# Hash and row sums in four column groups, eight hash transfers, and a second queue for one output piece

## The chip, the cores and the metric

The kernel runs on one core of one Trainium2 chip. The metric is the device time of one execution in microseconds (us). TensorE (PE in the profile) multiplies matrices, VectorE (DVE), ScalarE (ACT) and GpSimd (POOL) work on elements, and SyncE (SP), ScalarE and GpSimd start DMA transfers. Matrix results stand in PSUM, everything else in SBUF, both with 128 partitions.

## The reference

Attention in which a query sees only the keys of its own hash bucket, and then a two-layer network. Cut to what matters:

```
B, H, S, D = 4, 8, 768, 64;  proj: [64, 6]
q_bits = (q @ proj > 0);  k_bits = (k @ proj > 0)          # 6 bits for each row
mask   = bucket(q_bits)[..., :, None] == bucket(k_bits)[..., None, :]
scores = where(mask, (q @ k.T) / 8, -1e9)
attn   = softmax(scores);   x = (attn @ v)  ->  [3072, 512]
h = x @ w_in                                                # [3072, 2048]
out = (max(h, 0) + alpha * min(h, 0)) @ w_out               # [3072, 512]
```

All of it is float32 in the reference.

## The kernel before

The work has two blocks. The first is attention and lasts until about 318 us of the profile. It handles 16 pairs of heads (`pairs`, index `pi`), two heads at once: head s = 0 in partitions 0 to 63, s = 1 in partitions 64 to 127. The second is the network, a sequence of products in which seven products stand for eight (`Product`, L882).

The order is written out by hand: `do` keeps every instruction of an engine in the order of the program, so the order of calls in the loop at L1165 is the order on each engine. DMA starts stand on the queue of the engine that starts them: most loads and stores on SyncE, the weight loads `load_weight` (L578) and the hash transfers on GpSimd.

For a pair the loop does, on TensorE:

- `scores` (L760): 12 cells (six blocks of 128 keys times two halves of 384 queries). A cell has two bf16 matmuls of the hash rows (`bits`) and two f32 matmuls of q and k (`tr`), one of each for each head, into a PSUM tile `sc` of two banks. The hash part is 0 where all six bits agree and negative otherwise; ScalarE's Exp (L771) turns the cell into `pts`.
- `hash_bits` for the next pair (L713).
- `attend` (L793): the product with v, in tiles of 128 rows and 32 columns, four side by side, into `av`.
- `totals` (L807): the ones product. Row sums of `pts`, first added up by VectorE (`accp`, `accd`, L779 to L790), are multiplied with a matrix of ones into `sm`.

`two_banks` (L683) gives tiles of two PSUM banks from a ring of three. Scores, hash and totals all take from this ring, so the third cell of a pair gets the buffer of the `sm` tile before it.

On VectorE `divide` (L820) follows in the next pair's time: two transposes of `sm` into `st` (L831), the reciprocals (L834), the copies on GpSimd that exchange the halves (L840, L841), a transpose into `dn` and the product `x` (L849), which goes to DRAM. VectorE also turns q and k of later pairs (`turn_blocks`, L704) and prepares the network's weights (`weight_*`).

The hash in more detail. `wh` holds proj in columns 0 to 5 of a 32-column matrix, for each head in its 64 partitions. For pair `pi + 1`, eight matmuls of 64 rows by 32 columns (two heads, q and k, two halves of 384) fill both banks of one tile; a Sign on ScalarE with bias `hb` writes `kb` (L736), with 6 rows of signs and 6 rows of constants for each head and name. Rows then have to move to the partitions of their head: four transfers of 32 rows for q (L741) and two of 64 rows for k (L743), all started by GpSimd; one half of k is already in place. The first pair is done in another way, by halves, with its own tiles (`engine=DVE`), since its bits are needed at once.

At the end of the network `turn_out` (L1061) transposes a finished piece of the output on VectorE and starts twelve transfers of it on SyncE; `turn_last` (L1077) does the last two pieces with TensorE. A piece is put on the list `to_turn` in a product's last step (step 4). In the last block of the loop `turn_last(0)` is called where the other blocks call `turn_out`, and `turn_last(1)` after the loop.

Of the kernel before, what the change touches and what calls it, by code (L numbers as in the profile page):

```python
# [407 lines left out]
def fast_path(  # L408
# [12 lines left out]
    nc = tc.nc  # L421
# [39 lines left out]
    wh = const.tile([P, 32], F32, name="wh")  # L461
    hb = const.tile([P, 1], F32, name="hb")
    hb_k = const.tile([P, 2], F32, name="hb_k")
    alpha16 = const.tile([NF, P], F32, name="alpha16")
    alpha = const.tile([P, NF], F32, name="alpha")
    mags = const.tile([P, 2, NPAIR], F32, name="mags")

    qbs = [pool.tile([P, S], BF16, name=f"qb{i}", bufs=1) for i in range(2)]
    NI = NF // 2
    NM = 7  # L470
    w_in_s = dram.tile([NI, P, NM, 2, P], F32, name="w_in_s")
# [238 lines left out]
        n = "qk".index(name)  # L710
        do(ACT.activation(t, t, AF.Square, accum_out=mags[:, n, pi : pi + 1]))

    def hash_bits(pi, halves=BOTH, engine=None):  # L713

        if halves.start == 0:
            bits["q", pi] = qbs[pi % 2]
            kb = pool.tile([P, 3 * CW], BF16, name=f"kb{pi}", tag="kb", bufs=1)
            bits["k", pi] = kb[:, :S]  # L720
            bits["raw", pi] = kb.rearrange("p (a w) -> p a w", w=CW)
        ps = {"k": two_banks(f"hs{pi}")}
        ps["q"] = psum_av.tile([P, 2, 512], F32, name=f"hsq{pi}", tag="av") if engine is DVE else ps["k"]
        for half in range(halves.start, halves.stop):
            for name in "qk" if engine is DVE else "kq":
                for s in range(2):
                    r, c = D * s, D * (s ^ half) + 32 * "kq".index(name)

                    for t, c in [("k", c)] + ([("q", c ^ D)] if engine is DVE and name == "q" else []):
                        do(PE.matmul(  # L730
                            ps[t][c : c + 32, half if t == "k" or engine is not DVE else 0, :CW], wh[r : r + D],
                            tr[name, pi][r : r + D, half * CW : (half + 1) * CW], start=True, stop=True,
                        ))
        if engine is None:
            raw = bits["raw", pi]
# [8 lines left out]
            return  # L744
        for half in range(halves.start, halves.stop):
            cols = slice(half * CW, (half + 1) * CW)
            for s in range(2):
                c = D * (s ^ half ^ (engine is DVE)) + 32
                do(ACT.activation(
                    bits["q", pi][D * s : D * s + 32, cols], ps["q"][c : c + 32, 0 if engine is DVE else half, :CW], AF.Sign, bias=hb[c : c + 32],  # L750
                ))

            for to, c, n in [(0, 0, P)] if half == 0 else [(0, D, D), (D, 0, D)]:
                dst, src = bits["k", pi][to : to + n, cols], ps["k"][c : c + n, half, :CW]
                do(DVE.tensor_scalar(
                    dst, src, hb_k[c : c + n, 0:1], hb_k[c : c + n, 1:2], op0=ALU.is_gt, op1=ALU.subtract,
                ))


    def scores(pi, cells):  # L760
# [46 lines left out]
    def totals(pi):  # L807


        sums[pi] = two_banks(f"sm{pi}")  # L810
        for g in range(NCH):
            for s in range(2):
                for h in range(2):
                    r = D * s + 32 * h
                    do(PE.matmul(
                        sums[pi][r : r + 32, g, :HW2], ones, accd[pi][:, NCH * g + s, h * HW2 : (h + 1) * HW2],
                        start=True, stop=True,
                    ))

    def divide(pi, between=lambda: None):  # L820

        b, hp = pairs[pi]
        n = HW2 // 32
        a = pool.tile([P, NCH, HW2], F32, name=f"st{pi}", tag="st", bufs=1)
        r = pool.tile([P, NCH, n], F32, name=f"rc{pi}", tag="rc")
        rr = pool.tile([P, NCH, 2, n], F32, name=f"rr{pi}", tag="rr")
        d = pool.tile([P, NCH, CW], F32, name=f"dn{pi}", tag="dn", bufs=1)
        for g in range(NCH):  # L830
            do(DVE.transpose(a[:, g], sums[pi][:, g, :HW2]))  # L831
        do(DVE.tensor_scalar(r, a.rearrange("p g (n w) -> p g n w", w=32)[:, :, :, 0], S * EPS, None, op0=ALU.add))
        for h in range(2):
            do(DVE.reciprocal(rr[:, :, h], r))  # L834
        vsum[pi] = pool.tile([P, 1], F32, name=f"vs{pi}", tag="vs")
        do(DVE.tensor_scalar(vsum[pi], av[pi][:, 0, CW : CW + 1], EPS, None, op0=ALU.mult))
        weight_sums(1, vsum[pi])
        for q0 in (0, D):
            q1 = q0 + 32
            do(POOL.tensor_copy(rr[q0 : q0 + 32, :, 1], rr[q1 : q1 + 32, :, 1]))  # L840
            do(POOL.tensor_copy(rr[q1 : q1 + 32, :, 0], rr[q0 : q0 + 32, :, 0]))  # L841
        between()
        do(DVE.transpose(
            d.rearrange("p g w -> p (g w)"),
            rr.rearrange("p g h n -> p (g h n)").unsqueeze(2).to_broadcast([P, 2 * NCH * n, 32]),
        ))
# [295 lines left out]
    for half in (first, second):  # L1142
        turn(0, "q", half)
        turn(0, "k", half, DVE)
        if half is first:
            nil[0]()
            hash_bits(0, first, DVE)
    load(1, "q")
    load(1, "k")
    load_weight(0, nc.sync)  # L1150
# [178 lines left out]
```

## Time and profile before

| what | value |
| --- | --- |
| median of 3 runs | 875.19 us (874.47 to 875.37) |
| profiled execution, own time | 874.04 us |
| its span | 872.3 us |
| granted TensorE clock | 0.998 of full speed |
| TensorE busy | 861.0 us, 99% of the span |
| VectorE busy | 748.5 us, 86% |
| ScalarE busy | 366.8 us, 42% |
| GpSimd busy | 116.2 us, 13% |
| matmul records of the hash (L730) | 256, 29.2 us counted by record |
| matmul records of the ones product (L815) | 256, 13.5 us |
| Sign of the hash (L736) | 15, 901 ns each |
| transposes of the sums (L831) | 32, 343 ns each |
| issues of hash transfers (L741, L743) | 60 at 504 ns and 30 at 520 ns |

A line of the timeline gives the start and the length in us, engine, source line, operation, output<-input, and a count. A matmul of f32 leaves two records. "64*128" before a shape is the tile of TensorE (rows by columns); matmuls in different tiles may run side by side, and a length of 0.81 for four records is the time from the first start to the last end. "Idle before" is the time an engine stood still before an instruction, with what ended it. A wait in the list of waits has the total, the count and the longest.

### The profile page before, as it was taken

What the parts mean: (1) busy time and instruction counts of PE and PEld (TensorE: products, weight loads), DVE (VectorE), ACT (ScalarE), POOL (GpSimd) and SP (SyncE); (2) the same over time, 40 slices, a digit from 0 to 9 for tenths busy, and PEclk for the clock granted to TensorE, in tenths of its full rate; (3) what the DMA queues carried; (4) which work ended last, traced back from release to release, by engine and by line L of the source; (5) the groups of instructions that cost most, each with busy time, mean ns of one, the idle gap of its engine ahead of it and who ended that gap; (6) DMA issues with size and microseconds to landing.
All of it is one profiled execution on the core that took longest, in us unless ns stands there. A gap on an engine that the chain in (4) does not pass through costs nothing.

```text
span 872.3 us, 15248 instructions
## 1 busy us (share of the span) xinstructions
PE 861.0 (99%) x5706; PEld 575.2 (66%) x5706; DVE 748.5 (86%) x1215; ACT 366.8 (42%) x654; POOL 116.2 (13%) x249
## 2 busy tenths in 40 slices
PE   9999999999999999999999999999999999999996
PEld 4444444444444445569995559996558997557996
DVE  5999999999999987999897769897669889668985
ACT  7777888888777732221112221112222112222111
POOL 1322433323334310210000000000000000000000
PEclk9999999999999999999999999999999999999999
DMA  8865897798799446785434334343425333420242
GB/s 201 188 151 132 189 237 159 170 232 225 172 262 189 151 130 234 265 290 205 133 115 121 134 125 165 118 148 90 173 89 163 145 109 113 165 84 1 97 158 64
DMA packets 170820, 137.24 MB, mean 157 GB/s; under 512 B 126016, under 2 KB 154384, under 8 KB 167152
## 3 DMA queue, kind: packets, MB, share of 16 engines
q1 hardware_dynamic: 158960, 108.44, 43.9%
q0 software_dynamic: 9360, 26.55, 10.4%
q10 hardware_dynamic: 2416, 1.18, 0.5%
q8 instruction: 47, 0.77, 0.4%
q14 instruction: 37, 0.30, 0.1%
HBM read 104.87 MB, written 28.31 MB: 153 GB/s over the span
## 4 chain that ended last, share of the span: by engine, by line
PE 65%; DVE 1%; issue 1%; POOL 0%; ACT 0%; DVEq 0%
PE f_0a L902 2%; PE z_4a L902 2%; PE z_6a L902 2%; PE z_7a L902 2%; PE z_3a L902 2%; PE z_2a L902 2%; PE z_1a L902 2%; PE z_5a L902 2%; PE f_4a L902 2%; PE f_2a L902 2%; PE f_5a L902 2%; PE f_7a L902 2%; PE f_6a L902 2%; PE f_3a L902 2%; PE f_1a L902 2%; PE z_2c L902 1%
## 5 line engine op out<-in xcount | busy, mean ns | idle before, releaser
L768 PE MATMUL sc<-qT,kT 64*128 64x384 f32 x768 | 155.1, 482 | 0.0
L771 ACT ACTIVATE pt<-sc 128x768 f32<-128x768 f32 x192 | 153.1, 811 | 2.4 <-PE sc L768 1.1
L801 PE MATMUL av<-pt,vn 128*32 128x385 f32 (+1 forms) x1536 | 127.4, 486 | 0.0
L801 PEld LDWEIGHTS av<-pt,vn 128*32 128x32 f32 x1536 | 48.8, 109 | 77.4 <-issue 68.6
L768 PEld LDWEIGHTS sc<-qT,kT 64*128 64x128 f32 x768 | 68.2, 188 | 36.9 <-issue 36.4
L955 DVE TENSOR_TENSOR g<-g,g 128x384 f32<-128x384 f32 x128 | 68.3, 554 | 2.2
L768 PE MATMUL sc<-qb,kb 64*128 64x384 bf16 x384 | 63.1, 324 | 1.7 <-DVE st L831 1.4
L1019 DVE TENSOR_TENSOR gs<-g,gs 128x768 f32<-128x768 f32 x56 | 53.3, 951 | 1.0
L1011 DVE TENSOR_TENSOR ws<-wl 128x512 f32<-128x512 f32 x56 | 38.4, 686 | 17.8 <-DMA wl<-w_out_s 16.0
L1019 DVE TENSOR_TENSOR gs<-g 128x768 f32<-128x768 f32 x56 | 53.2, 950 | 0.0
L596 ACT ACTIVATE wr<-raw 128x512 int32<-128x512 uint32 x32 | 22.2, 692 | 58.0 <-issue 34.1
L951 DVE SCALAR_TENSOR_TENSOR g<-h,alpha 128x384 f32<-128x384 f32 x32 | 19.7, 616 | 25.2 <-ACT h L944 25.1
L768 PEld LDWEIGHTS <-kb 64*128 64x128 bf16 x384 | 19.6, 94 | 32.6 <-issue 6.6
L779 DVE TENSOR_TENSOR accp<-pt,pt 128x1536 f32<-128x1536 f32 x16 | 28.1, 1758 | 9.9 <-ACT pt L771 9.9
L741 POOL DMA_DIRECT2D qb<-kb x60 | 30.0, 504 | 29.8 <-ACT kb L736 29.8
L784 DVE TENSOR_TENSOR accd<-accd,pt 128x1536 f32<-128x1536 f32 x16 | 28.1, 1758 | 1.7
L790 DVE TENSOR_TENSOR accd<-accd,accp 128x1536 f32<-128x1536 f32 x16 | 28.1, 1758 | 0.6
L787 DVE TENSOR_TENSOR accp<-accp,pt 128x1536 f32<-128x1536 f32 x16 | 28.0, 1753 | 0.0
L783 DVE TENSOR_TENSOR accd<-pt,pt 128x1536 f32<-128x1536 f32 x16 | 28.0, 1750 | 0.0
L902 PE MATMUL f_0a<-x,wi 128*128 128x384 f32 x64 | 23.5, 489 | 0.0
L902 PE MATMUL f_2a<-x,wi 128*128 128x384 f32 x64 | 23.3, 486 | 0.0
L902 PE MATMUL f_1a<-x,wi 128*128 128x384 f32 x64 | 23.3, 486 | 0.0
(357 smaller groups left out, 1759.9 us busy)
## 6 DMA issues: line engine op xcount, KB each, us to landing
wi<-w_in_s SPq DMA_DIRECT2D x32, 896.0 KB, 4.7
wl<-w_out_s SPq DMA_DIRECT2D x16, 1024.0 KB, 4.8
wl<-w_out_r SPq DMA_DIRECT2D x12, 1024.0 KB, 4.9
raw<-in_moe_w_in_dram POOLq DMA_DIRECT2D x15, 512.0 KB, 5.1
raw<-in_moe_w_out_dram POOLq DMA_DIRECT2D x14, 512.0 KB, 4.7
w_in_s<-wsi SPq DMA_DIRECT2D x16, 448.0 KB, 6.7
qn<-in_q_dram SPq DMA_DIRECT2D x64, 96.0 KB, 5.7
vn<-in_v_dram SPq DMA_DIRECT2D x16, 384.0 KB, 5.8
```

What stands on the lines that cost most here:

```text
L741: nc.gpsimd.dma_start(bits["q", pi][D * s : D * s + 32, cols], raw[c + 32 : c + 64, 2 * half])
L768: do(PE.matmul(sc[:, s, :CW], what["k", pi][r, ks], what["q", pi][r, qs], start=first, stop=not first,))
L771: do(ACT.activation(pts[kc][:, g, :, :CW], sc[:, :, :CW], AF.Exp, scale=SCALE / DOWN))
L779: do(DVE.tensor_tensor(accp[pi], p(0), p(1), op=ALU.add))
L783: do(DVE.tensor_tensor(accd[pi], p(3), p(4), op=ALU.add))
L784: do(DVE.tensor_tensor(accd[pi], accd[pi], p(5), op=ALU.add))
L790: do(DVE.tensor_tensor(accd[pi], accd[pi], accp[pi], op=ALU.add))
L801: do(PE.matmul(av[pi][D * s + t : D * s + t + 32, g, :w], nat["v", pi][:, s, kc * D + t : kc * D + t + 32], pts[kc][:, g, s, :w], start=(k ...
L902: do(PE.matmul(self.ps[bank], self.left(left, k), self.right(right, k), start=start and k == 0, stop=k == self.nk - 1, skip_group_check=no ...
L955: do(DVE.tensor_tensor(new_g(b, to)[:, i], g_m[b, x][:, i], g_m[b, y][:, i], op=ALU.subtract))
L1011: do(DVE.tensor_tensor(t, w2[b, n, x], w2[b, n, y], op=op))
L1019: do(DVE.tensor_tensor(t, g2[b, n, x], g2[b, n, y], op=ALU.subtract))
```

## The change

1. **Hash, pairs 1 to 15.** A new weight matrix `wh2` of 128 rows by 32 columns holds proj twice: in columns 0 to 5 for the partitions of head 0, in columns 12 to 17 for those of head 1, zero elsewhere. One matmul of 128 rows then hashes both heads. Four matmuls (k and q, two halves) of 384 columns go to the four column groups of one PSUM bank, in place of eight in two banks. The Sign covers 128x384 in place of 128x768 and writes a new tile `hr`.
2. **Placing the rows.** Eight transfers of 12 rows by 384 columns bring them from `hr` to `qb` and `kb`, in place of six of 32 or 64 rows. `kb` becomes one fixed tile. Rows that aren't written hold zeros in `qb`.
3. **Setup.** `setup_hash` adds sixteen small instructions on VectorE after the second half of the first pair's hash. The first pair's hash itself (`hash_first`) issues what it issued before.
4. **Ones product.** Four matmuls of 384 columns into four column groups of one bank, in place of eight of 192 columns in two banks; `divide` transposes them in one instruction of 128x384, in place of two of 128x192, and the small tiles `r` and `rr` lose an axis.
5. **An output piece.** In `turn_out`, the middle one of every three transfers of piece 5 of the last batch goes to GpSimd's queue.

```diff
+    def setup_hash():
+        do(DVE.memset(wh2, 0.0))
+        for s in range(2):
+            do(DVE.tensor_copy(wh2[D * s : D * s + D, 2 * NB * s :][:, :NB], wh[D * s : D * s + D, :NB]))
+        do(DVE.memset(hb2, 0.0))
+        for r in range(0, P, 32):
+            for n, x in ((3, -1e-37), (2, -1.0 if r < D else 1.0), (1, -1e-37)):
+                do(DVE.memset(hb2[r : r + n * NB], x))
+
+    def hash_bits(pi):
+        ps = two_banks(f"hs{pi}")[:, 0, :CW]
+        for half in range(2):
+            for n, name in enumerate("kq"):
+                c = D * n + 32 * half
+                do(PE.matmul(
+                    ps[c : c + 32], wh2, tr[name, pi][:, half * CW : (half + 1) * CW], start=True, stop=True,
+                ))
+        raw = pool.tile([P, CW], BF16, name=f"hr{pi}", tag="hr", bufs=1)
+        do(ACT.activation(raw, ps, AF.Sign, bias=hb2))
+        bits["q", pi], bits["k", pi] = qbs[pi % 2], kb
+        for half in range(2):
+            for n, name in enumerate("kq"):
                 for s in range(2):
...
-            do(ACT.activation(raw[:, 0:3:2], ps["k"][:, :, :CW], AF.Sign, bias=hb))
-            for half in range(2):
-                for s in range(2):
-                    c = D * (s ^ half)
-                    cols = slice(half * CW, (half + 1) * CW)
-                    nc.gpsimd.dma_start(bits["q", pi][D * s : D * s + 32, cols], raw[c + 32 : c + 64, 2 * half])
-                    if half:
-                        nc.gpsimd.dma_start(bits["k", pi][D * s : D * s + D, cols], raw[c : c + D, 2])
...
+                    c = D * n + 32 * half + NB * s
+                    nc.gpsimd.dma_start(
+                        bits[name, pi][D * s : D * s + 2 * NB, half * CW : (half + 1) * CW], raw[c : c + 2 * NB],
+                    )
...
             for s in range(2):
-                for h in range(2):
-                    r = D * s + 32 * h
-                    do(PE.matmul(
-                        sums[pi][r : r + 32, g, :HW2], ones, accd[pi][:, NCH * g + s, h * HW2 : (h + 1) * HW2],
-                        start=True, stop=True,
-                    ))
+                r = D * s + 32 * g
+                do(PE.matmul(
+                    sums[pi][r : r + 32, 0, :CW], ones, accd[pi][:, NCH * g + s], start=True, stop=True,
+                ))
...
-        for g in range(NCH):
-            do(DVE.transpose(a[:, g], sums[pi][:, g, :HW2]))
-        do(DVE.tensor_scalar(r, a.rearrange("p g (n w) -> p g n w", w=32)[:, :, :, 0], S * EPS, None, op0=ALU.add))
-        for h in range(2):
-            do(DVE.reciprocal(rr[:, :, h], r))
+        do(DVE.transpose(a, sums[pi][:, 0, :CW]))
+        do(DVE.tensor_scalar(r, a.rearrange("p (n w) -> p n w", w=32)[:, :, 0], S * EPS, None, op0=ALU.add))
         for g in range(NCH):
+            do(DVE.reciprocal(rr[:, g], r))
...
-                    nc.sync.dma_start(
+                    queue = nc.gpsimd if (b, p) == (B - 1, 5) and c % 2 else nc.sync
+                    queue.dma_start(
...
-    hash_bits(0, second, DVE)
+    hash_first(1)
     scores(0, ahead[1:])
+    setup_hash()
     turn_blocks(1, "q")
```

More of the change, by code (lines that the diff above doesn't have):

```diff
@@ L463, in fast_path @@
     hb_k = const.tile([P, 2], F32, name="hb_k")
+    wh2 = const.tile([P, 32], F32, name="wh2")
+    hb2 = const.tile([P, 1], F32, name="hb2")
     alpha16 = const.tile([NF, P], F32, name="alpha16")
@@ L468, in fast_path @@
     qbs = [pool.tile([P, S], BF16, name=f"qb{i}", bufs=1) for i in range(2)]
+    kb = pool.tile([P, S], BF16, name="kb", bufs=1)
     NI = NF // 2
@@ L711, in magnitude @@
         do(ACT.activation(t, t, AF.Square, accum_out=mags[:, n, pi : pi + 1]))
[L713 to L725, printed above, removed]
-                for s in range(2):
[L727 to L732, printed above, removed]
-                        ))
-        if engine is None:
-            raw = bits["raw", pi]
-            do(ACT.activation(raw[:, 0:3:2], ps["k"][:, :, :CW], AF.Sign, bias=hb))
-            for half in range(2):
-                for s in range(2):
-                    c = D * (s ^ half)
-                    cols = slice(half * CW, (half + 1) * CW)
-                    nc.gpsimd.dma_start(bits["q", pi][D * s : D * s + 32, cols], raw[c + 32 : c + 64, 2 * half])
-                    if half:
-                        nc.gpsimd.dma_start(bits["k", pi][D * s : D * s + D, cols], raw[c : c + D, 2])
-            return
-        for half in range(halves.start, halves.stop):
-            cols = slice(half * CW, (half + 1) * CW)
-            for s in range(2):
[L748 to L757, printed above, removed]
@@ new lines, in hash_first @@
+    def hash_first(half):
+        bits["q", 0], bits["k", 0] = qbs[0], kb
+        ps = {"k": two_banks("hs0"), "q": psum_av.tile([P, 2, 512], F32, name="hsq0", tag="av")}
+        cols = slice(half * CW, (half + 1) * CW)
+        for name in "qk":
+            for s in range(2):
+                r, c = D * s, D * (s ^ half) + 32 * "kq".index(name)
+                for t, c in [("k", c)] + ([("q", c ^ D)] if name == "q" else []):
+                    do(PE.matmul(
+                        ps[t][c : c + 32, half if t == "k" else 0, :CW], wh[r : r + D],
+                        tr[name, 0][r : r + D, cols], start=True, stop=True,
+                    ))
+        for s in range(2):
+            c = D * (s ^ half ^ 1) + 32
+            do(ACT.activation(
+                bits["q", 0][D * s : D * s + 32, cols], ps["q"][c : c + 32, 0, :CW], AF.Sign, bias=hb[c : c + 32],
+            ))
+        for to, c, n in [(0, 0, P)] if half == 0 else [(0, D, D), (D, 0, D)]:
+            do(DVE.tensor_scalar(
+                bits["k", 0][to : to + n, cols], ps["k"][c : c + n, half, :CW], hb_k[c : c + n, 0:1],
+                hb_k[c : c + n, 1:2], op0=ALU.is_gt, op1=ALU.subtract,
+            ))
@@ L812, in totals @@
             for s in range(2):
-                for h in range(2):
-                    r = D * s + 32 * h
-                    do(PE.matmul(
-                        sums[pi][r : r + 32, g, :HW2], ones, accd[pi][:, NCH * g + s, h * HW2 : (h + 1) * HW2],
-                        start=True, stop=True,
-                    ))
+                r = D * s + 32 * g
+                do(PE.matmul(
+                    sums[pi][r : r + 32, 0, :CW], ones, accd[pi][:, NCH * g + s], start=True, stop=True,
+                ))
     def divide(pi, between=lambda: None):
         b, hp = pairs[pi]
[L825 to L828, printed above, removed]
+        n = CW // 32
+        a = pool.tile([P, CW], F32, name=f"st{pi}", tag="st", bufs=1)
+        r = pool.tile([P, n], F32, name=f"rc{pi}", tag="rc")
+        rr = pool.tile([P, NCH, n], F32, name=f"rr{pi}", tag="rr")
         d = pool.tile([P, NCH, CW], F32, name=f"dn{pi}", tag="dn", bufs=1)
+        do(DVE.transpose(a, sums[pi][:, 0, :CW]))
+        do(DVE.tensor_scalar(r, a.rearrange("p (n w) -> p n w", w=32)[:, :, 0], S * EPS, None, op0=ALU.add))
         for g in range(NCH):
-            do(DVE.transpose(a[:, g], sums[pi][:, g, :HW2]))
-        do(DVE.tensor_scalar(r, a.rearrange("p g (n w) -> p g n w", w=32)[:, :, :, 0], S * EPS, None, op0=ALU.add))
-        for h in range(2):
-            do(DVE.reciprocal(rr[:, :, h], r))
+            do(DVE.reciprocal(rr[:, g], r))
         vsum[pi] = pool.tile([P, 1], F32, name=f"vs{pi}", tag="vs")
@@ L839, in divide @@
             q1 = q0 + 32
-            do(POOL.tensor_copy(rr[q0 : q0 + 32, :, 1], rr[q1 : q1 + 32, :, 1]))
-            do(POOL.tensor_copy(rr[q1 : q1 + 32, :, 0], rr[q0 : q0 + 32, :, 0]))
+            do(POOL.tensor_copy(rr[q0 : q0 + 32, 1], rr[q1 : q1 + 32, 1]))
+            do(POOL.tensor_copy(rr[q1 : q1 + 32, 0], rr[q0 : q0 + 32, 0]))
         between()
@@ L844, in divide @@
             d.rearrange("p g w -> p (g w)"),
-            rr.rearrange("p g h n -> p (g h n)").unsqueeze(2).to_broadcast([P, 2 * NCH * n, 32]),
+            rr.rearrange("p g n -> p (g n)").unsqueeze(2).to_broadcast([P, NCH * n, 32]),
         ))
@@ L1146, in fast_path @@
             nil[0]()
-            hash_bits(0, first, DVE)
+            hash_first(0)
     load(1, "q")
```

## The prediction

> **What bounds the kernel.** I read the page first (parts 1 and 2), then the TensorE timeline of one attention period, then the waits and the VectorE timeline where TensorE pauses.
>
> ```profile
> PE 861.0 (99%) x5706; PEld 575.2 (66%) x5706; DVE 748.5 (86%) x1215; ACT 366.8 (42%) x654; POOL 116.2 (13%) x249
> PE   9999999999999999999999999999999999999996
> DVE  5999999999999987999897769897669889668985
> ```
>
> TensorE is busy to the end and VectorE nearly so in the first third. The change touches only that third, so its periods decide. One period, 202.16 to 221.31, is 19.15 us; its second half, in the TensorE timeline (start, length, instruction, count):
>
> ```profile
> 211.22 0.81 PE L768 MATMUL sc<-qT,kT 64*128 64x384 f32 x4
> 211.96 0.51 PE L730 MATMUL hs<-kT,wh 64*32 64x384 f32 x2
> ...
> 212.34 0.49 PE L730 MATMUL hs<-qT,wh 64*32 64x384 f32 x2
> 212.76 7.96 PE L801 MATMUL av<-pt,vn 128*32 128x385 f32 x96
> 220.54 0.84 PE L815 MATMUL sm<-accd,ones 128*32 128x192 f32 x16
> 221.31 0.34 PE L768 MATMUL sc<-qb,kb 64*128 64x384 bf16 x2
> ```
>
> No gap: scores 9.80, hash 0.80, attend 7.78, ones 0.77. In this window VectorE is busy for 17.94 us of 19.15. So a shorter piece of TensorE work here shortens the period, until VectorE is late. It already is at the first, and at the last three, boundaries between pairs:
>
> ```profile
> PE sc L768 <- DVE st L831: 1.4, 3, 0.6
> PE sm L815 <- DVE accd L790: 0.2, 1, 0.2
> ```
>
> There the third score cell of a pair waits until the two transposes at L831 have released the buffer of the ones product.
>
> **Hash product, fifteen times.** A matmul of f32 leaves two records. The eight 64x32 matmuls start their first records from 211.96 and their second from 212.31, all eight side by side; attend starts at 212.76. So today's eight are one set, not two, and halving their number doesn't halve 0.80. What the four new ones cost is read from attend: 48 matmuls of the same shape (128 rows, 32 columns, 384 wide), four at a time, take 220.54 - 212.76 = 7.78, or 0.648 a set (0.324 a record step). The hash step costs more than that because it is entered from and left to other tile shapes: 0.35 for its first step and 0.45 for its second. New hash: 0.35 on entering + 0.322 = 0.67, since attend has the same tile shape; attend's own first step, 0.35 today, becomes 0.322. Gain 0.13 + 0.03 = 0.16 us each. Bounds: 0 if leaving costs what it does now, 0.19 if entering becomes cheaper too. I take 0.16, because 23 of attend's 24 steps show it.
>
> The Trainium skill, TensorEngine Tiling (Array Packing), "Theoretical Speedup", says that a contraction of at most 64 gains up to 2x from row tiles, which the change gives up. By that the hash would go to 1.6 us and the kernel lose 0.8 in each bound period (8.8 in eleven). The rows above speak against it: the new weights fill all 128 rows with both heads, and a 128-row set takes 0.648.
>
> **Ones product, sixteen times.** Two sets of 192 columns take 0.77 (four record steps of 0.162 and the way out); one set of 384 has two steps of 0.322. Gain 0.00 to 0.01; the column steps are the same sum.
>
> **VectorE.** Two transposes of 128x192 take 0.60 (timeline at 202.59); the row for one of 128x384 is L1066 at 0.555. Gain 0.05 per pair. The two reciprocals, the add, and the GpSimd copies keep their element counts: nothing. setup_hash adds sixteen small instructions between the last kb piece of pair 0 and the turning of pair 1. Small memsets stand 0.09 to 0.11 apart in the setup rows (L537, L538, L543), the copies are taken at the 0.15 of L540: 12 x 0.107 + 0.06 + 0.1 + 2 x 0.12 = 1.7 us. Its cover:
>
> ```profile
> 11.55 0.98 DVE L704 STREAM_TRANSPOSE qT<-qn 128x768 f32<-128x768 f32 x1
> 13.38 0.98 DVE L704 STREAM_TRANSPOSE kT<-kn 128x768 f32<-128x768 f32 x1 [0.85 <-DMA kn<-in_k_dram]
> 15.16 0.43 DVE L598 TENSOR_SCALAR wx<-raw 128x512 uint32<-128x512 uint32 x1 [0.80 <-DMA raw<-in_moe_w_out_dram]
> ```
>
> The two DMA waits hold 1.65 us. qT would start at 13.25, kT at 14.15 and end before 15.16, when the weight arrives. Cost 0; if the sixteen take 2.0, it is 0.2, because from 15.16 VectorE works without a pause until the first boundary.
>
> **ScalarE.** Sign over 128x384 in place of 128x768 (L736, 0.90): about 0.45 shorter, half of it by elements. Behind it wait the GpSimd transfers; ScalarE itself is idle for 3.5 us later in the period, so alone it is worth nothing. But the magnitudes run 0.45 earlier, and with them the q loads of 128-byte elements.
>
> **Transfers.** Six issues (0.50 and 0.52 each) become eight. In the period above they run from 214.19 to 217.24; the new ones would run from 213.75 to 217.75. The built order shows the needs: the first score cell waits for issues 1 to 4, the second for issues 7 and 8, which is at 221.31 + 0.82 - 0.16 = 221.97. The fence gives issue to landing of the query transfers, smallest, middle and largest, over all periods:
>
> ```profile
> DMA to landing us min/median/max: 1.6/3.7/6.4
> ```
>
> Issued at 217.25, the last lands at 218.9 to 220.95 with the first two; 6.4 would be late, but it occurs behind a weight load: the largest, in the period that starts at 106.43, belongs to an issue at 118.45, landing with the five after it at 124.85, 125.04, 125.22, 125.40, 125.61, 126.18, behind four stores of w_in_s. There, and after 163.87 (181.83 to 183.69; scores at 183.02), the second cell's need (126.2 and 183.7 after the change) leaves 0 to -0.5 for two more pieces in that file. The new pieces are 9 KB, the old 24 and 48. Bounds per period 0 and 0.6; I take 0.1 each, 0.2 in all, nearer to 0 because the new pieces hold less than half of the bytes.
>
> The Trainium skill, DMA: Bandwidth & Descriptors, "Anatomy of one DMA", fits 2.0 us plus the bytes for each GpSimd DMA. One after another, eight would take 16 us, estimated from that page, and the scores would wait 8 us in every period. The landings above are 0.2 apart, so the fixed part overlaps.
>
> **A new wait.** In the built order each GpSimd transfer waits for the one eight back on its semaphore. There are now ten issues per pair, so the eighth hash piece waits for the weight load issued just before the hash. Behind it on GpSimd stand the next weight load, the wsi sums and the rr copies; TensorE's second cell waits for the piece itself. That load (211.38 in the period above) lands after 5.7, at 217.06, before the eighth issue at 217.25. Only in the two congested periods, and by 0.5 in one other, is it later (121.73 against 121.5, 180.60 against 179): inside the 0.2 above.
>
> **The last turned piece.** Piece 5 of the last batch is finished in the step before the last, and the last step calls turn_last, not turn_out. The new queue choice is never met; the built SyncE order is unchanged. 0.
>
> **Sum**, against the profiled execution (874.04; its span 872.3). Hash gains count where TensorE is bound: the eleven periods of pairs 1 to 11, 11 x 0.17 (with 0.01 of the ones product) = 1.87. In pairs 0, 12, 13, 14 the next boundary waits for VectorE, so only its 0.05 counts: 0.20. In the bound ones the third cell has room: transposes end at 203.20 for a cell at 203.79; 0.59 becomes 0.47. Then -2.07 + 0.2 = -1.87, which the second block, all TensorE, carries to the end. The median of the runs is 875.19, 1.15 above the profiled one, and I shift by the same: 873.3. A measurement tells about 0.2% (1.75 us, so 873.44), and this lies just beyond that line.
>
> **Rivals.** (1) Work counts: half the matmuls, half the hash time, and the ones likewise: 15 x 0.40 + 16 x 0.3 = 11, so 864. The side-by-side starts speak against it. 0.03. (2) The way from one product to the next costs what it costs, whatever the shape, or VectorE becomes the bound at once: only 0.2 to 0.6 gained, 874.8. For it: 17.94 of 19.15 and the four late boundaries; against it: 0.59 of room. 0.22. (3) Slower: the last two of eight pieces land after the second cell needs them in ordinary periods. Room there is 221.97 - 217.25 = 4.7, so it decides from a landing of 4.7 us, or an issue of 0.65 in place of 0.50 with the middle landing of 3.7. At 1 us late in half of fifteen periods, +7.5 less 1.8: 881; at 0.5, 877. For it: 4.5 us and more occurs in six of fifteen periods; against it: those were late behind a weight load issued earlier, so late issues share its end. 0.13. Forecast: 0.62.
>
> **Chances.** The forecast's own range is 872.8 to 874.2: at one end 0.20 in each of eleven periods, 0.20 at the boundaries and no waits (2.4), at the other 0.13, 0.20 and 0.3 in each congested period (1.03). Its middle is close to the line; I put three quarters of it on the fast side, since the waits are its softest term and the smaller pieces speak against them. Faster 0.03 + 0.47 = 0.50; same 0.15 + 0.22 = 0.37; slower 0.13. The range goes from 872.6 (0.2 below for the spread of the runs, 874.47 to 875.37) over rival 2 to 875.6, and leaves out rivals 1 and 3.
>
> **What would show it.** Hash start to attend start 0.67 (not 0.80) in every period; bound periods of 18.98; ones still 0.77; one transpose near 0.55; VectorE's first weight instruction still at 15.2; pairs 13 to 15 still with the third cell late. It is wrong if TensorE's second score cell waits for a qb transfer in ordinary periods, if hash to attend stays at 0.80, or if sm waits for accd everywhere.

## The result, and the profile after

| kernel | median of six runs | from to | ratio to before [95%] |
| --- | --- | --- | --- |
| before | 874.64 us | 874.40 to 875.37 | 1 |
| changed | 879.70 us | 877.71 to 880.61 | 1.0055 [1.0044, 1.0065] |

The change makes the kernel 5 us slower; 873.3 was forecast. The profiled execution took 880.52 us, its span is 878.6, the granted clock 0.995. Line numbers are now those of the changed kernel: hash L732, Sign L736, hash transfers L742, scores L781, attend L814, ones product L827, sums L792 to L803, transpose of the sums L841.

Parts 1 and 2 of the page:

```profile
PE 861.8 (98%) x5458; PEld 577.3 (66%) x5458; DVE 749.9 (85%) x1215; ACT 361.4 (41%) x654; POOL 130.4 (15%) x279
PE   9999999999998999999999999999999999999996
DVE  6999989989997987999888769898668988668986
```

TensorE has 248 records fewer and is yet busy for 861.8 us, as before (861.0): its busy time alone tells nothing (records at a lower clock count as busy for longer, see below). The one 8 that is new in its row is slice 13, at 264 to 286 us: a hole in a place where there was none.

The TensorE timeline of an ordinary period, second half:

```profile
213.92 0.81 PE L781 MATMUL sc<-qT,kT 64*128 64x384 f32 x4
214.66 0.51 PE L732 MATMUL hs<-kT,wh 128*32 128x384 f32 x1
...
215.02 0.49 PE L732 MATMUL hs<-qT,wh 128*32 128x384 f32 x1
215.33 7.94 PE L814 MATMUL av<-pt,vn 128*32 128x385 f32 x96
223.08 0.83 PE L827 MATMUL sm<-accd,ones 128*32 128x384 f32 x8
223.84 0.34 PE L781 MATMUL sc<-qb,kb 64*128 64x384 bf16 x2
```

Here the forecast holds to the hundredth: hash to attend 0.67 (was 0.80), ones product 0.76, and a period of 18.98 us (was 19.15). Of the fourteen periods from hash start to hash start eight take 18.98 and a ninth takes 19.14 (19.31 before). What was lost stands in the list of TensorE's waits:

```profile
PE sc L781 <- DMA qb<-hr: 5.6, 3, 3.2
...
PE sm L827 <- DVE accd L803: 1.0, 1, 1.0
PE sc L781 <- DVE st L841: 0.8, 2, 0.6
```

The first line is new. Its three waits are before the first cell of pair 6 and before the second cells of pairs 9 and 13 (TensorE timeline, three places; in brackets the idle time and what ended it):

```profile
126.68 0.43 PE L781 MATMUL sc<-qb,kb 64*128 64x384 bf16 x2 [0.92 <-DMA qb<-hr]
...
186.71 0.32 PE L781 MATMUL sc<-qb,kb 64*128 64x384 bf16 x1 [1.46 <-DMA qb<-hr]
...
266.13 0.48 PE L781 MATMUL sc<-qb,kb 64*128 64x384 bf16 x1 [3.18 <-DMA qb<-hr]
266.13 1.75 PE L781 MATMUL sc<-qT,kT 64*128 64x384 f32 x4
267.57 0.63 PE L781 MATMUL sc<-qb,kb 64*128 64x384 bf16 x2
```

The third wait costs more than its 3.18 us. After it four f32 records take 1.75 us and two bf16 records 0.63, for 0.81 and 0.33 in the ordinary period: TensorE's granted clock is 0.50 from 266.1 to 269.1 us, 0.89 in the next microsecond and 1.00 after that. From 266.13 to the next hash (276.66) TensorE waits for nothing more, and yet needs 10.53 us; the variant with the set-up moved (below) needs 8.97 for the same stretch, at a clock of 1.00. So the low clock costs some 1.6 us.

On GpSimd's timeline the eighth hash transfer of the same three periods is issued late, each time after an idle stretch:

```profile
122.69 0.50 POOL L742 DMA_DIRECT2D qb<-hr  x1 [0.83 <-DMA raw<-in_moe_w_out_dram]
...
182.08 0.50 POOL L742 DMA_DIRECT2D qb<-hr  x1 [1.81 <-DMA raw<-in_moe_w_in_dram]
...
262.31 0.50 POOL L742 DMA_DIRECT2D qb<-hr  x1 [4.34 <-issue]
```

The first two name the weight load issued just before the hash (`raw`); it landed at 122.41 and 181.80, 0.28 us before. For the third the profile names nothing ("issue"): that load had landed at 259.10, 3.21 us before. The wait alone is not the loss: in pair 5 the eighth piece waits too (issued at 103.90, its load landed at 103.62), but it lands at 106.46, before the second cell at 107.53. The summary of all issues of L742, to set beside 1.6/3.7/6.4 of before, has a shorter middle and a longer end:

```profile
DMA to landing us min/median/max: 1.5/3.1/7.8
```

The wait of `sm` is that of pair 0's ones product for VectorE. VectorE's timeline of the opening:

```profile
14.00 0.98 DVE L707 STREAM_TRANSPOSE qT<-qn 128x768 f32<-128x768 f32 x1
14.90 0.94 DVE L707 STREAM_TRANSPOSE kT<-kn 128x768 f32<-128x768 f32 x1
15.76 0.38 DVE L601 TENSOR_SCALAR wx<-raw 128x512 uint32<-128x512 uint32 x1
...
25.40 1.76 DVE L797 TENSOR_TENSOR accd<-accd,pt 128x1536 f32<-128x1536 f32 x1 [0.53 <-ACT kn L714]
```

The two DMA waits of before are gone: the set-up (12.01 to 14.00, 1.99 us) has used them up. And there is an idle 0.53 us before the third sum that was not there.

From hash start to hash start, in the profiled executions (us). A period has the name of the pair whose scores lie in it, except the first, which is called pair 0 after its ones product. The prediction's sum counts by the ones product throughout: its pairs 12 and 13 are pairs 13 and 14 here.

| kernel | pair 0 | pair 6 | pair 9 | pair 13 | pair 14 | the nine others |
| --- | --- | --- | --- | --- | --- | --- |
| before | 20.38 | 19.15 | 19.15 | 19.50 | 19.91 | 19.15 |
| changed | 20.91 | 20.46 | 20.75 | 24.05 | 19.42 | 18.98 |
| difference | +0.53 | +1.31 | +1.60 | +4.55 | -0.49 | -0.17 each, -1.5 in all |

(The first of the nine others is 19.31 before and 19.14 after.)

With +0.42 before the first hash (the opening varies by that much from execution to execution, see below) the sum is +6.4 (the profiled executions differ by 6.48, the medians by 5.06). The last attend starts at 315.80 instead of 309.35; from there to the end it is 562.84 us in the changed kernel and 562.90 in the one before. So all of it is lost in attention: in four periods, and 0.42 us ahead of the first hash.

### The profile page after: what moved, and what is told of

Same layout as the page of the kernel before. It is cut to its first block, busy times and chain, and to the rows that moved or that the text cites. A ratio compares the mean times of both kernels' runs of the same rounds, so it can differ in the third digit from the quotient of the medians.

```text
span 878.6 us, 14811 instructions
## 1 busy us (share of the span) xinstructions
PE 861.8 (98%) x5458; PEld 577.3 (66%) x5458; DVE 749.9 (85%) x1215; ACT 361.4 (41%) x654; POOL 130.4 (15%) x279
## 4 chain that ended last, share of the span: by engine, by line
PE 61%; DVE 4%; issue 1%; POOL 0%; ACT 0%; DVEq 0%; ACTq 0%
PE f_0a L912 2%; PE z_4a L912 2%; PE z_7a L912 2%; PE z_3a L912 2%; PE z_6a L912 2%; PE z_5a L912 2%; PE f_4a L912 2%; PE f_3a L912 2%; PE f_2a L912 2%; PE f_1a L912 2%; PE z_2a L912 2%; PE f_5a L912 2%; PE z_1a L912 2%; PE f_7a L912 2%; PE f_6a L912 2%; PE z_2c L912 1%
## 5 line engine op out<-in xcount | busy, mean ns | idle before, releaser
L781 PE MATMUL sc<-qT,kT 64*128 64x384 f32 x768 | 157.4, 487 | 0.0
L814 PE MATMUL av<-pt,vn 128*32 128x385 f32 (+1 forms) x1536 | 127.0, 485 | 0.0
L814 PEld LDWEIGHTS av<-pt,vn 128*32 128x32 f32 x1536 | 50.3, 109 | 73.8 <-issue 71.7
L781 PEld LDWEIGHTS sc<-qT,kT 64*128 64x128 f32 x768 | 70.6, 189 | 41.4 <-issue 40.5
L781 PE MATMUL sc<-qb,kb 64*128 64x384 bf16 x384 | 66.7, 325 | 6.9 <-DMA qb<-hr 5.6
L781 PEld LDWEIGHTS <-kb 64*128 64x128 bf16 x384 | 22.0, 94 | 35.5 <-issue 12.3
L792 DVE TENSOR_TENSOR accp<-pt,pt 128x1536 f32<-128x1536 f32 x16 | 28.2, 1760 | 16.6 <-ACT pt L784 16.6
L742 POOL DMA_DIRECT2D kb<-hr x60 | 30.3, 507 | 24.1 <-ACT hr L736 23.5
L742 POOL DMA_DIRECT2D qb<-hr x60 | 29.8, 500 | 8.0 <-issue 4.3
L797 DVE TENSOR_TENSOR accd<-accd,pt 128x1536 f32<-128x1536 f32 x16 | 28.1, 1759 | 2.1 <-ACT kn L714 0.5
L803 DVE TENSOR_TENSOR accd<-accd,accp 128x1536 f32<-128x1536 f32 x16 | 28.1, 1758 | 0.6
L912 PE MATMUL f_4a<-x,wi 128*128 128x384 f32 x64 | 23.3, 486 | 0.0
```

Source lines behind the costliest of these rows:

```text
L742: nc.gpsimd.dma_start(bits[name, pi][D * s : D * s + 2 * NB, half * CW : (half + 1) * CW], raw[c : c + 2 * NB],)
L781: do(PE.matmul(sc[:, s, :CW], what["k", pi][r, ks], what["q", pi][r, qs], start=first, stop=not first,))
L792: do(DVE.tensor_tensor(accp[pi], p(0), p(1), op=ALU.add))
L797: do(DVE.tensor_tensor(accd[pi], accd[pi], p(5), op=ALU.add))
L803: do(DVE.tensor_tensor(accd[pi], accd[pi], accp[pi], op=ALU.add))
L814: do(PE.matmul(av[pi][D * s + t : D * s + t + 32, g, :w], nat["v", pi][:, s, kc * D + t : kc * D + t + 32], pts[kc][:, g, s, :w], start=(k ...
```

## The experiments

**Theory A**: a GpSimd transfer waits for the landing of the one eight back on its queue. With ten per pair the last hash piece, which the second score cell needs, waits for the weight load issued just before the hash. **Theory B**: the pieces are late by sheer traffic, whoever waits for whom. **Theory C**: the opening and its variation. Edits are against the changed kernel unless said otherwise.

### Which piece goes last

```diff
-        for half in range(2):
-            for n, name in enumerate("kq"):
+        for half, n, name in ((0, 0, "k"), (0, 1, "q"), (1, 1, "q"), (1, 0, "k")):
```

> The changed kernel with the eight hash transfers in another order: the second half's two query pieces go fifth and sixth, its two key pieces seventh and eighth, so the piece that is issued last is one that the seventh cell of the scores is the first to read (some 3 us of score cells later), not the second. Theory A (a GpSimd transfer waits for the landing of the one eight back on its queue, which for the last piece is now the weight load issued just before the hash, and the second cell waits for it): the waits before the second cell in the periods of pairs 6, 9 and 13 (1.5, 1.5 and 3.2 us) go or shrink to under 0.5 each, because the two query pieces are then held only by transfers that landed long ago; some of pair 13's may come back at the seventh cell, as its last piece was issued 4.3 us after the seventh. Attention's end moves earlier by 3 to 6 us and the time is 874 to 877 us. Theory B (the queue is longer and its 12-row pieces land late by sheer traffic, whoever waits for what): the order matters little, the waits only move to a later cell, and the time stays at 878.5 to 880.5. Theory C (the loss is the start-up and run-to-run variation): also 878.5 to 880.5, with the waits before the second cell gone and nothing gained.

Measured: 874.35 us, 0.9997 [0.9988, 1.0007] of before. Periods: pair 6 19.71, pair 9 18.98, pair 13 19.56. Of the waits for a hash piece one is left (TensorE timeline):

```profile
126.33 0.44 PE L781 MATMUL sc<-qb,kb 64*128 64x384 bf16 x2 [0.56 <-DMA qb<-hr]
```

The last piece still waits for the weight load; only now nobody needs it so soon. An edit that moves no byte and adds or removes no transfer takes back 5 us, so A holds and C falls as the main cause. B is left with pair 6, where 0.73 us remain: there all eight pieces, issued from 118.36, landed only from 125.8 on, behind the weight load and other traffic.

### Two pieces on another queue

```diff
-                    nc.gpsimd.dma_start(
+                    queue = nc.scalar if (half, n) == (1, 1) else nc.gpsimd
+                    ins = queue.dma_start(
...
+                    if queue is nc.scalar:
+                        do(ins)
```

> The changed kernel with the last two query pieces of each pair issued from ScalarE's queue rather than GpSimd's: GpSimd then has eight transfers for each pair (two weight loads, six hash pieces), as before the change. Theory A: no piece that the second cell needs waits for a weight load any more; the stalls of pairs 6, 9 and 13 (1.5, 1.5, 3.2 us) go; against it ScalarE spends some 0.1 to 0.5 us per issue between the Sign and its next Exp, hidden or not; 874 to 877 us. Theory B (traffic): the same eight pieces move the same rows, the landings stay late in the same three periods, 878.5 to 880.5. Theory C (start-up, variation): 878.5 to 880.5.

Measured: 873.70 us, 0.9991 [0.9981, 1.0000]. Pair 6 19.61, pair 9 18.98, pair 13 19.59; no second cell waits. With eight GpSimd transfers per pair the wait is gone. The two issues take mostly 0.73 us each on ScalarE's queue, more than was expected, and no cost of them shows.

### The ones product alone

The kernel before, with the new ones product and the divide that reads it:

```diff
+                r = D * s + 32 * g
+                do(PE.matmul(
+                    sums[pi][r : r + 32, 0, :CW], ones, accd[pi][:, NCH * g + s], start=True, stop=True,
+                ))
```

> The kernel before with the ones product, its column groups and the divide that reads them as in the changed kernel, and nothing else of the change (hash, transfers and the last turned piece as before). My sum: the ones product is worth 0 to 0.01 us per pair, one transpose of 128x384 instead of two 128x192 about 0.05 us of VectorE per pair, both off the path: 874.2 to 875.0, the same as before within 0.2%. If the ones product is what costs (its waits for the accumulators stand at 1.0 us, three times, in the changed kernel), this kernel is slower by 1 to 5 us.

Measured: 875.03 us, 1.0004 [0.9995, 1.0013]. It is worth nothing either way, as summed.

### Two more transfers in the old hash

The kernel before, with two transfers of 24 rows ahead of the six pieces, and the second half's query pieces last:

```diff
+            for s in range(2):
+                nc.gpsimd.dma_start(extra[D * s : D * s + 2 * NB], raw[D * s : D * s + 2 * NB, 0])
```

> The kernel before with two more GpSimd transfers per pair, 24 rows of 384 from the Sign's output into a tile that nothing reads, issued ahead of the six hash pieces; of the six, the second half's query pieces go last. So GpSimd has ten transfers per pair as after the change, and the last is the query piece that the second cell needs, eight behind the weight load issued just before the hash; products, Sign and VectorE work are those of before. Theory A: the second cell waits for that piece in the periods where the weight load is slow to land, as in the changed kernel: 1 to 5 us slower than before, 876 to 880. Theory B (only the small 12-row pieces or the changed products cost): within 1 us of before, 874 to 875.5.

Measured: 970.89 us, 1.1096 [1.1074, 1.1118], far outside both expectations. GpSimd's timeline shows why: the scheduler, which places GpSimd's transfers, put the next weight load ahead of the last piece.

```profile
209.95 0.57 POOL L583 DMA_DIRECT2D raw<-in_moe_w_out_dram  x1 [2.77 <-DVE wx L638]
...
211.94 0.51 POOL L746 DMA_DIRECT2D qb<-kb  x1
```

The load waits for VectorE to free its buffer, the piece stands behind it, and the second cell waits in every pair (list of TensorE's waits):

```profile
PE sc L773 <- DMA qb<-kb: 66.3, 15, 7.6
```

So it is no clean test of A. It shows what it costs when the second cell's piece stands behind a long wait: 4.4 us of waiting in each of fifteen pairs (66.3 over 15). The whole loss is more, 96.3 us, and a lower clock is in it: in the period of the lines above the second cell waits for 5.18 us until 217.09, and TensorE's granted clock is then 0.50 from 217 to 222 us. The mean clock of this kernel is 0.956.

### The set-up moved

```diff
+        do(DVE.memset(wh2, 0.0))            # in setup(), with the other constants
+        do(DVE.memset(hb2, 0.0))
...
-            do(DVE.tensor_copy(wh2[...], wh[...]))
+            do(POOL.tensor_copy(wh2[...], wh[...]))
```

> The changed kernel with the hash's set-up elsewhere: its fourteen memsets stand with the other small constants in the opening (VectorE idle from 2.7 to 6.1 us there) and its two copies of the projection go to GpSimd, so nothing of it is on VectorE between the first pair's second hash half and the first block turn. Theory A (the set-up's 1.99 us on VectorE is not covered: it moves the turns, the weight step and the accumulator sums of pair 0 by up to 1 us, since the ones product waits for the sum): the second hash starts at 39.1 to 39.5 us instead of 40.0, everything else as in the changed kernel, and the time falls by 0.5 to 0.9 us, to some 878.9. Theory B (pair 0's later end is start-up variation): the second hash still starts at 39.8 to 40.1, no gain, 879.7. The stalls of pairs 6, 9 and 13 should stay in both, so the total may move by up to 1.5 us either way through them; the start of the second hash decides.

Measured: 878.46 us, 1.0040 [1.0027, 1.0053]. Pair 0 20.67 instead of 20.91. The start that the expectation speaks of is that of the last score matmul before the second hash: 39.76 us (40.02 in the changed kernel), between the two, nearer to B. The idle 0.53 us before the third sum is gone, but VectorE's first weight instruction starts at 15.88, after a wait of 0.55 for the weight itself. Over all kernels here it starts at 15.0 to 16.0, so pair 0 varies by that much with or without the set-up.

### Sixteen instructions ahead on GpSimd

```diff
+    for _ in range(16):
+        do(POOL.memset(shift, 0.0))
```

> The changed kernel with sixteen one-element-per-partition memsets on GpSimd after the first pair's hash, before its loop: they do nothing but move GpSimd's later instructions by sixteen places in its program. In the changed kernel, and in the one with the key pieces last, the eighth transfer of pair 13 was issued 3.2 to 3.5 us after the landing it waits for, where every other period shows 0.28. Theory A' (that extra time is GpSimd's own program running over an edge of its fetched code, at that place by chance): the extra 3.2 us are gone from pair 13's eighth transfer and stand at another instruction some sixteen places earlier in that program, most likely before the weight load or the copies of pair 12; the pair's scores take 11 to 12 us instead of 14.9, and the time falls by 2 to 4 us, to 876 to 878. Theory B' (it belongs to pair 13's place in the work: a release by VectorE or TensorE that comes then): the eighth transfer of pair 13 stays 3 us late and the time stays 878.5 to 880.5.

Measured: 879.35 us, 1.0045 [1.0031, 1.0060]. The late issue of pair 13 did not move (GpSimd timeline; the load had landed at 258.43):

```profile
261.64 0.50 POOL L742 DMA_DIRECT2D qb<-hr  x1 [4.70 <-issue]
```

It is again 3.21 us after the landing. So theory A' is refuted: sixteen instructions more do not move the place.

### The weight load behind the pieces

```diff
-        load_weight(i + 4)
         if pi + 1 < NPAIR:
             hash_bits(pi + 1)
+        load_weight(i + 4)
+        if pi + 1 < NPAIR:
```

> The changed kernel with the weight load that stands just ahead of each hash moved behind it on GpSimd: the eight pieces are issued first, then the 256 KB load. The transfer eight back from the last piece is then the earlier weight load of the period, landed some 14 us before. Theory A (the last piece waits for the landing of the transfer eight back): the waits before the second cell in pairs 6, 9 and 13 go, and with the pieces ahead of the load in the queue the first cell of pair 6 no longer waits either (their landing within 2 to 3 us of issue); attention ends 6 to 7 us earlier, 873 to 874. The load comes some 4 us later each time; if its weight step needs it at once, VectorE's and ScalarE's weight work slips and gives back up to 2 us. Theory B (traffic): landings of the pieces stay at 5 to 7 us in those periods, 877 to 880.

Measured: 881.83 us, 1.0080 [1.0064, 1.0097]. The edit did nothing: for transfers outside `do` the place in the source does not set the order, and GpSimd's built program still has the load first. So this is the changed kernel a second time, and its median is 2.1 us above that of the first (879.70): a difference of that size between kernels that stall can't be put down to an edit. Whether the order itself would help was not tried.

> Both of the last two edits at once: weight load behind the eight pieces, and the hash's set-up in the opening and on GpSimd. If the two account for all that the forecast missed, what is left is the shorter way between the products, 0.165 us in each of twelve to fourteen periods, and the time is 872.3 to 873.2, 1.5 to 2.3 us under the kernel before. If the late periods (14 and 15) are set by VectorE's sums rather than by TensorE, they give nothing and it is 872.8 to 873.6. If neither edit matters it is 878 to 880.

This one (both edits) is for the same reason the kernel with the moved set-up a second time. Measured: 879.18 us, 1.0045 [1.0032, 1.0058]; pair 0 20.33. Taken together, the set-up in place costs 0.24 and 0.57 us in pair 0 (20.91 against 20.67, 20.90 against 20.33), which is less than the 1.2 and 2.7 us of the medians. Of the rest most that the profiled executions show stands in pair 13 (24.05 and 23.40 against 21.72 and 21.76), and there the clock differs. In the kernel with 23.40 the second cell waits for 2.41 us, and TensorE's granted clock is 0.57 in the 4 us after that; in the two with the moved set-up it waits for 2.42 and 2.46 us, and the clock stays at 1.00. What decides that is not shown.

### Counting GpSimd's transfers

In six kernels with ten transfers per pair the late issue had been the same one: GpSimd's 129th transfer since the start. With the two weight loads of pair 0 on SyncE:

```diff
-        load_weight(i + 3)
+        load_weight(i + 3, nc.sync if pi == 0 else nc.gpsimd)
...
-        load_weight(i + 4)
+        load_weight(i + 4, nc.sync if pi == 0 else nc.gpsimd)
```

> The changed kernel with the two weight loads that GpSimd issues for pair 0 issued by SyncE instead; from pair 1 on GpSimd issues the same ten transfers per pair in the same order. Counted over the whole program, the transfer that went late in pair 13 of every kernel with ten per pair was GpSimd's 129th, its issue 2.93 us later than the landing it waits for explains, also with sixteen instructions ahead of it; in the kernel before, the 129th is a write of the output weights after attention, and its idle time is 2.93 us longer there (3.89) than before the same write of the changed kernel (0.96). Theory A'' (every 128 GpSimd transfers one more costs 2.9 us, whatever it is): pair 13's last piece is now the 127th and is issued 0.3 us after its landing; the 129th is the weight load just before the hash of pair 14, and that one is late, covered by its wait for ScalarE. Period 14 falls from 24.1 us to 20 to 21.2, the time from 879.7 to 876 to 877.5. Theory B'' (it belongs to pair 13's place): period 14 stays at 21.7 to 25 us and the time at 878.5 to 882. The waits of pairs 6 and 9 stay in both.

Measured: 876.22 us, 1.0015 [1.0006, 1.0024]; pair 13 19.43, less than expected. The eighth piece of pair 13, now the 127th, goes 0.28 us after its load landed (257.05); the 129th is the load just before the hash of pair 14 (GpSimd timeline):

```profile
257.33 0.52 POOL L742 DMA_DIRECT2D qb<-hr  x1 [0.46 <-DMA raw<-in_moe_w_out_dram]
...
274.71 0.58 POOL L585 DMA_DIRECT2D raw<-in_moe_w_out_dram  x1 [7.04 <-ACT wx L603]
```

GpSimd is idle for 7.04 us before this load, and for 4.09 before the same load in the kernel before (4.11 with the key pieces last): it goes 2.9 us late as well, and costs nothing. Pair 9's stall (19.87) stays, as theory A has it.

Then the reverse, in the kernel before: twenty-three small transfers early on, which bring the 129th to the first hash piece made in pair 13.

```diff
+            for n in range(0 if pi > 8 else 2 if pi == 1 else 3):
+                nc.gpsimd.dma_start(extra[32 * n : 32 * n + 2 * NB], raw[32 * n : 32 * n + 2 * NB, 0])
```

> The kernel before with twenty-three more GpSimd transfers of twelve rows into a tile that nothing reads, behind the hash pieces of the first eight pairs after the opening's; nothing else is changed, and from then on GpSimd's program is that of before. They bring the 129th GpSimd transfer to the first query piece of the hash that pair 13 makes for pair 14, issued at 271.97 us in the kernel before, 0.96 us after GpSimd's last work, as soon as the Sign is done. Theory A'' (the 129th GpSimd transfer goes 2.9 us late, whatever it carries): that piece is issued 2.9 us later against the Sign's end, 3.9 us of GpSimd idle instead of 0.96, and the five pieces behind it as well; they land some 2 to 5 us after, at or up to 2 us past the first cell of pair 14; the time is 874.8 to 877. The write of the output weights that was the 129th before has 0.96 us of idle instead of 3.89. Theory B'' (it belonged to the changed kernel's pair 13, and 3.89 against 0.96 is chance): the piece goes at its time and the time is 874.5 to 875.

Measured: 875.20 us, 1.0002 [0.9992, 1.0012]. GpSimd's timeline of this kernel, the piece and, after attention, the write that was the 129th before:

```profile
274.90 1.50 POOL L742 DMA_DIRECT2D qb<-kb  x3 [3.90 <-ACT qn L712]
...
359.15 0.76 POOL L999 DMA_DIRECT2D w_out_s<-wo  x1 [0.96 <-DVE wo L998]
```

The same write in the kernel before, where it is the 129th:

```profile
362.35 0.76 POOL L996 DMA_DIRECT2D w_out_s<-wo  x1 [3.89 <-DVE f_4p L947]
```

and in the changed kernel, where it is not:

```profile
365.59 0.76 POOL L1006 DMA_DIRECT2D w_out_s<-wo  x1 [0.96 <-DVE wo L1005]
```

3.90 - 0.96 = 2.94 and 3.89 - 0.96 = 2.93; in the changed kernel 3.21 - 0.28 = 2.93 again. Shown, then: in these kernels the 129th GpSimd transfer goes 2.9 us late, be it a hash piece, a load or a write of weights. Here it cost nothing, because the pieces landed at 278.28 to 279.46 and the scores began at 279.14. Why it goes late stays open.

### The cures together

> The changed kernel with the last two query pieces issued by ScalarE (GpSimd back to eight transfers per pair) and the hash's set-up in the opening and on GpSimd: the two cures together. With both, what is left of the change is 0.165 us per period in twelve periods (2.0), less 0.6 in pair 6 where all pieces land late behind other traffic, and nothing in pairs 13 and 14, where VectorE's sums end last: 872.8 to 873.6, faster than the kernel before by 1.0 to 1.8 us. If the set-up in place costs nothing (its 0.5 us of VectorE idle before the third sum being there anyway), 873.5 to 874.

Two pieces on ScalarE and the moved set-up. Measured: 874.39 us, 0.9993 [0.9984, 1.0002]: no better than the two pieces alone (873.70). Pair 0 is 21.11 (21.07 there), its weight instruction starts at 15.74 after 1.28 us of waiting for the weight. The gain of the moved set-up is not shown here.

> The changed kernel with three edits: the two key pieces of the second half last, the set-up in the opening and on GpSimd, pair 0's two loads on SyncE. All issues of the pieces stay on GpSimd. Theory A with A'': no wait before a second cell is left, pair 6's first cell waits some 0.6 to 0.8 us, 873 to 874. If holding the queue (the piece that waits for a weight load also holds the weight load behind it) matters as such, VectorE's weight steps come later in periods 6, 9 and 13 and it is 874 to 875.5.

Measured: 873.47 us, 0.9984 [0.9975, 0.9994]. This is the one version whose whole interval lies below the kernel before, by a narrow margin (medians 873.47 and 874.77). Pair 9 18.98, pair 13 19.43, and in pair 6 (19.99) the first cell still waits:

```profile
126.07 0.43 PE L781 MATMUL sc<-qb,kb 64*128 64x384 bf16 x2 [0.84 <-DMA qb<-hr]
```

The two profiled executions are at the upper end of their runs (877.02 and 876.02); both have a wait of about 1 us for a weight load in the network, which the changed kernel's does not show. Part of the spread of a median lies there, outside the change.

## Why the prediction was wrong

**The step that failed is "A new wait".** The mechanism stood there: the eighth piece waits for the weight load just before the hash, and two of the late landings were listed (121.73 against an issue at 121.5, 180.60 against 179). They were then priced by how late the issue would be, up to 1.6 us, and put "inside the 0.2" as if the piece could still land with its neighbours. But its own issue to landing comes after the wait: in pair 9 issue 182.08 plus 4.59 gives 186.67, and the cell wanted it at 185.25. The right sum is landing of the load, plus 0.28, plus the 4.6 to 5.3 us that such an issue takes in these periods, against the need of the second cell. Measured: 1.77 us in pair 9 (20.75 against 18.98) and some 0.75 in pair 6 (20.46 against 19.71 with the key pieces last), where 0.2 stood for everything.

**Pair 13 was no term at all.** Its load's landing alone would have left the piece near its need (259.10 + 0.28 + 3.8 = 263.2; the cell wanted it at 262.94). The 2.93 us of the 129th transfer made it the largest loss: TensorE stood still for 3.18 us, and the half clock after that took some 1.6 us more, which no term held either. With 4.55 us this period is the greater part of the miss. No line of the kernel before pointed to it but the 3.89 of one write, which was idle time of an engine off the path.

**Smaller misreadings.** The list of late loads has two more in the kernel before: by the same spacing, pair 1's (landed at 25.99, eighth issue at 25.2) and pair 14's (276.39 against 275.0). No second cell of these two pairs waits for a piece in the changed kernel. And at the last boundary between pairs the profile names ScalarE (0.3 us), not VectorE. The Sign became 0.32 us shorter (0.90 to 0.58), not 0.45; no loss comes from that.

**"Transfers"**: 0.1 for each congested period was too little in one: in pair 6 all eight pieces land late, 0.6 to 1.0 us, in the four kernels where no query piece stands behind a weight load any more (19.61 to 19.99). After 163.87 (pair 9) nothing is lost once the new wait is out of the way: 18.98 with the key pieces last.

**"VectorE", the set-up**: sixteen instructions took 1.99 us instead of 1.7, and the cover of 1.65 was used up as the prediction had it. Its "0.2 if they take 2.0" became 0.24, 0.57 and -0.04 in the three pairs of kernels that differ by nothing else (the third is 21.07 against 21.11, with two pieces on ScalarE). The part that no sum could hold is the idle 0.53 us before the third sum.

**Right**: the hash (0.17 us per period: 18.98 for 19.15 in eight periods, 19.14 for 19.31 in a ninth), the ones product, the transposes (0.54 for 0.60), the bound by VectorE in pairs 13 and 14 (19.4 to 20.1 with the new hash where nothing stalls, 19.50 and 19.91 before), and the last turned piece (0; GpSimd issues 30 transfers more than before, two for each hash, and none of the output). The loss of 8.8 us, estimated from the 2x for small contractions of the Trainium skill, TensorEngine Tiling (Array Packing), "Theoretical Speedup", did not come: the hash takes 0.67.

**Rival 3** had the right sign, the right cell and the right engine. But it was argued for ordinary periods, where the last piece has 4.7 us of room; there it landed in time, in nine periods out of nine. That its 877 and 881 lie on either side of 879.7 is luck: it summed small delays in half of all periods, and the loss came from three. Rival 1 is refuted by the 0.67 and the 0.76, rival 2 by the 0.67 and the periods of 18.98.

Of the whole, 873.3 against 879.7: the nine ordinary periods gave what was summed (1.5); the three stalled ones and pair 0 took 8.0 (1.31 + 1.60 + 4.55 + 0.53).

## What to carry to other kernels

When an edit adds transfers to a queue, write down for each which earlier one it now waits for, and price the wait as the landing of that one plus a full issue to landing of its own, in the worst period and not in the typical one. Put the piece that is needed last at the end of the queue: that order cost nothing here and was worth 5 us. Count a long wait of TensorE for more than itself where it comes back at half clock: 1.6 us more in pair 13. A change that wins 0.17 us in each period can be lost in three of them, so add up the periods one by one.

## What the hardware showed that was not expected

- GpSimd's 129th transfer of a program was issued 2.93 to 2.95 us later than what it waits for explains: a hash piece in the changed kernel and in five variants with the same count, a write in the kernel before and in three variants with its count, a load in the two with pair 0's loads on SyncE, a hash piece in the one with twenty-three more. Sixteen instructions ahead of it changed nothing, two transfers fewer moved it. What happens there was not found.
- TensorE's granted clock was 0.50 to 0.57 in the 3 to 6 us after a wait of 3.18, 3.32 and 2.41 us in pair 13 (the changed kernel, the one with sixteen instructions more, the one with the load's call moved) and 1.00 after waits of 2.42 and 2.46 us at the same place. So the length of the wait alone does not tell whether the clock falls.
- In the changed kernel and in every variant with the set-up in place, VectorE stood idle for 0.53 us before the third sum of pair 0 (L797 of the changed kernel, at 25.0 to 25.6 us). The profile names ScalarE in five of these six kernels and VectorE's own previous sum in the sixth, so nothing that it shows explains it. It is absent in the kernel before and where the set-up's memsets stand in the opening. Those still have fourteen of the sixteen instructions ahead of the sum on VectorE, so a count of instructions alone does not explain it; its cause is open.
- Entering the four 128x32 tiles of the hash from the 64x128 tiles of the scores took 0.34 us for the first step, going on to attend's tiles of the same shape 0.33 (214.66, 215.00, 215.33).
